# Top-k attention and Fourier mixing on one Trainium2 core: the tail tokens' product moved ahead of the seven half products, and the attention output turned by DMA and normalised on GpSimd

## The chip, the cores and the metric

The kernel runs on one core of a Trainium2 chip. The core has five engines with a queue each: TensorE (PE in the profile; its weight loads are shown as PEld), VectorE (DVE), ScalarE (ACT), GpSimd (POOL) and SyncE (SP), which in this kernel issues nearly all DMA transfers. An engine executes its own instructions in the order in which the program lists them; between engines only semaphores order the work. The metric is the device time of one execution in microseconds, and the median of several runs stands for a kernel.

## The reference

The inputs `q`, `k`, `v` have the shape (8, 8, 576, 64): batch, head, token, channel. All is float32.

```python
scores = scale * np.matmul(q, k.transpose(0, 1, 3, 2))
kth = np.partition(scores, -32, axis=-1)[..., -32:-31]
scores = np.where(scores >= kth, scores, -1e9)
attn = np.exp(scores - np.max(scores, axis=-1, keepdims=True))
attn = attn / (np.sum(attn, axis=-1, keepdims=True) + 1e-09)
x = np.matmul(attn, v)                     # then heads side by side: (8, 576, 512)
mixed = np.real(np.fft.fft(np.fft.fft(x, axis=1), axis=2))
u = x + mixed
un = (u - mean(u)) / np.sqrt(var(u) + 1e-06)
out = u + np.maximum(un @ w_ch1, 0.0) @ w_ch2        # 512 -> 2048 -> 512
```

So each batch has an attention that keeps the 32 largest scores of a row, a two-dimensional Fourier transform of which only the real part is kept, and a two-layer network.

## The kernel before, in words

**Items and steps.** Heads are handled in pairs, four pairs to a batch, 32 in all. The 576 tokens of a head are cut into tiles of 128 rows (tiles 0 and 1 of the first half, 2 and 3 of the second) and a tile 4 with the last 32 tokens of each half, 64 rows. A pair has nine items, one for each tile and head, and one for tile 4 with both heads stacked. The loop at the end of the kernel (L1492 to L1631) takes one item a step, 36 steps a batch, 288 in all. In step i the program lists: the scores of item i+3 (`scores`, L334), the finding of the 32 largest of item i on VectorE (`top_ops`, L407: four MAX8 and three MATCH_REPLACE8), the threshold on GpSimd (`bounds`, L430), the masking of item i-1 (`mask`, L445: one ScalarE pass and one GpSimd subtraction), its exponential (`expo`, L455), and the following of item i-2.

**Two ways to turn the probabilities.** The product with v needs the probabilities with keys on the partitions. For the first batch and two pairs more TensorE turns them (`transposes`, L511). For the others (`pair_by_dma`, L438: pairs 4 to 30 without 7) ScalarE writes the float32 words apart into a plane of low and a plane of high 16-bit halves (`plane`, L466), SyncE writes these to DRAM and one step later reads them back with a transposing DMA, which works on 16-bit elements (`turn`, L494). The tile `PT` that results is used one or two steps later.

**From the attention to x.** `attend` (L555) multiplies `PT` with v into one PSUM bank `o` (pool `ps_o`, a single buffer): 20 instructions for each chunk. A chunk is ch 0 (tiles 0, 1, 4; 320 columns) or ch 1 (tiles 2, 3; 256 columns), so each pair has two. The result has channels on the partitions. `attended` (L573) copies it with ScalarE to `xT` (L578) and prepares the reciprocal of the sums, `rd` (L590, L591). `to_tokens` (L594) turns `xT` with one TensorE transpose a tile (L604) into `tpx`, which takes the same bank as `o`, and multiplies by `rd` on the way into `x`: on VectorE (L608, L615), or, in batch 1 for all but its last chunk, on ScalarE in the next step (`normalise_on_act`, L627). The queue `pending` says which chunk is due; `to_tokens` may run only when the batch two before has been stored, since `x` has two buffers.

**The Fourier transform of batch b** is done among the steps of batch b+1: folds on GpSimd (`fold_ops`, `fold_tails`), products with tables (`dft_tokens`, `dft_channels`), statistics, and turning the normalised u (`channels_first`). Their steps are written out by hand (L1378 to L1438) through `at(step, place, fn)`.

**The network of batch b** is a list of units (`mlp_units`, L952) that the loop deals out among the steps of batches b+1 and b+2: each step has a budget (`level`, L1465) from an estimate of the fixed work of TensorE (`fixed_cost`, L1452), and `some` (L1482) takes units while there is room. A chunk has 16 units `hidden` (L957: eight instructions each). For the second layer there are two ways. `back` (L986) multiplies a tile plainly: eight units for a tile of 128 tokens, four for tile 4 (L1032, whose two halves of the contraction go to two halves of the output rows and are added in `tails_done`, L1041). The other way, for ch 0 of batches 1 to 6 and both chunks of batch 7, is `fast` (L1068): tiles 0 and 1 against the four quarters of `w2` in seven half-size products instead of eight, `p2, p1, p5, p4, p6, p3, p7`, two units each (L1163, 16 instructions a product). It needs sums of the hidden activations on GpSimd (`mix`, L1108) and differences of the quarters of `w2`, which lie in DRAM (`w_parts`, shown as T1 to T4) and are brought over two quarters of `w2` itself in SBUF (`bring`, L909, 512 KB for each half): `begin` brings T1 over the quarter `w2_12`, then p2 brings T4 over `w2_21`, p5 brings T2, p4 brings T3, and at last p6 and p7 bring back the quarters themselves, B12 and B21. Whatever reads `w2` plainly must come before T1 or after B12 and B21. The order of the units for such a chunk is:

```python
begin, products = fast(ch)                # products[0] is a mix, no TensorE work
units.insert(1 - NIT, begin)              # after the first hidden unit
units += products
for t in [t for t in CHUNKS[ch] if t == 4 or not seven]:      # tile 4 comes here
    units += [ ... back(ch, t, p) for p in range(4 if t == 4 else 8) ]
```

Then follow the 16 hidden units of ch 1 and the plain products of tiles 2 and 3. Results are added to `x` by GpSimd (L1135, queued in `sums` and emitted by `some_sums` as room allows) or VectorE (L1121), and stored from there. `tails_done` calls `need((b, 0, "x", 4))`, which emits the queued sums up to that one, because it reuses the space of their operand.

**Banks.** Products of the network and of the Fourier transform share three PSUM banks in a rotating list (`bank`, L130). A product of the second layer holds its bank until the VectorE operation that ends it has been listed, at the end of the next step (`late_next`).

**SyncE's queue** takes in a step: the transposing read of item i-3, the planes of item i-2, what the units bring, loads of q, k and v, stores.

Of the kernel before, what the change touches and what calls it, by code (L numbers as in the profile page):

```python
# [9 lines left out]
F32 = mybir.dt.float32  # L10
# [63 lines left out]
def kernel(  # L74
# [363 lines left out]
    def pair_by_dma(pair):  # L438

        return NPB <= pair < NPAIR - 1 and pair != 2 * NPB - 1  # L440

    def by_dma(i):
        return pair_by_dma(i // PER_PAIR)

# [128 lines left out]
    def attended(pair, ch, late):  # L573

        o, w = o_of.pop((pair, ch)), CW[ch]
        PT.pop((pair, ch))
        xT = attp.tile([P, CW[0]], F32, name=f"xT_{pair}_{ch}", tag="xT", bufs=4)
        nc.scalar.copy(out=xT[:, 0:w], in_=o[:, 0:w])  # L578
        xT_of[pair, ch] = xT
        den = den_t[pair % 3]  # L580
        if ch == 0:
            for h in range(2):
                nc.scalar.copy(
                    out=den[TH * h:TH * (h + 1), 5:6],
                    in_=den[TAIL + TH * h:TAIL + TH * (h + 1), 4:5],
                )
        c0, n = (0, 6) if ch == 0 else (6, 4)
        rd = small.tile([P, 6], F32, name=f"rd_{pair}_{ch}", tag="rd", bufs=6)

        nc.scalar.activation(out=rd[:, 0:n], in_=den[:, c0:c0 + n], func=AF.Copy, bias=1e-9)  # L590
        late.append(lambda: nc.vector.reciprocal(out=rd[:, 0:n], in_=rd[:, 0:n]))  # L591
        rd_of[pair, ch] = rd

    def to_tokens(pair, ch, at_once=True):  # L594

        b, hp = divmod(pair, NPB)
        if b not in x_of:
            x_of[b] = batp.tile([P, 5, DM], F32, name=f"x_{b}", tag="x", bufs=2)
        x = x_of[b]
        xT, rd = xT_of.pop((pair, ch)), rd_of.pop((pair, ch))  # L600
        shape, name = [P, 4, P], f"tpx_{pair}_{ch}"
        tp = ps_o.tile(shape, F32, name=name, tag="o") if at_once else bank(shape, name)
        for n, t in enumerate(CHUNKS[ch]):
            nc.tensor.transpose(tp[0:ROWS[t], n, :], xT[:, P * n:P * n + ROWS[t]], ident)  # L604
        cols = slice(P * hp, P * (hp + 1))

        def normalise():
            nc.vector.tensor_tensor(  # L608
                out=x[:, 2 * ch:2 * ch + 2, cols].rearrange("p t (e d) -> p t e d", e=2),
                in0=tp[:, 0:2, :].rearrange("p t (e d) -> p t e d", e=2),  # L610
                in1=rd[:, 0:4].rearrange("p (t e) -> p t e", e=2).to_broadcast([P, 2, 2, D]),
                op=ALU.mult,
            )
            if ch == 0:
                nc.vector.tensor_tensor(  # L615
                    out=x[0:TAIL, 4, cols].rearrange("p (e d) -> p e d", e=2),
                    in0=tp[0:TAIL, 2, :].rearrange("p (e d) -> p e d", e=2),
                    in1=rd[0:TAIL, 4:6].to_broadcast([TAIL, 2, D]),
                    op=ALU.mult,
                )  # L620

        def normalise_on_act():
            for n, t in enumerate(CHUNKS[ch]):
                r = slice(0, ROWS[t])
                for e in range(2):
                    hd = slice(D * e, D * (e + 1))
                    nc.scalar.mul(  # L627
                        out=x[r, t, cols][:, hd], in_=tp[r, n, hd],
                        mul=rd[r, 2 * n + e:2 * n + e + 1],
                    )  # L630


        if b == 1 and (hp, ch) != (NPB - 1, 1):
            at(now[0] + 1, "act", normalise_on_act)
        else:
            (late_now if at_once else late_next).append(normalise)
        return 0.14 * len(CHUNKS[ch])
# [314 lines left out]
    def mlp_units(b):  # L952
# [16 lines left out]
                )  # L969
            nc.scalar.activation(out=hT_of[ch][:, it, :], in_=hp[:, 0:w], func=AF.Relu)  # L970

        cps, cts, stored = {}, [], []

        def ct_of(t):

# [10 lines left out]
        def back(ch, t, part):  # L986
            n, hT, rs = CHUNKS[ch].index(t), hT_of[ch], rs_of[b]
            if part == 0:
                cps[t] = bank([P, DM], f"cp_{b}_{t}", True)
            cp, free = cps[t]  # L990
            if t != 4:
                for it in range(2 * part, 2 * part + 2):
                    nc.tensor.matmul(  # L993
                        cp, lhsT=hT[:, it, P * n:P * (n + 1)], rhs=w2[:, it, :],
                        start=(it == 0), stop=(it == NIT - 1),
                    )
                if part == 7:
                    xt = x[:, t, :]

                    def store():  # L1000
                        tok = HS * (t // 2) + P * (t % 2)
                        nc.sync.dma_start(out=out[b, tok:tok + P, :], in_=xt)
                        stored.append(t)
                        if len(stored) == 4:
                            written.add(b)

                    def finish():
                        nc.vector.scalar_tensor_tensor(
                            out=xt, in0=cp, scalar=rs[:, t:t + 1], in1=xt, op0=ALU.mult, op1=ALU.add
                        )  # L1010
# [12 lines left out]

                    if last:
                        store()
                    else:
                        at(now[0] + 2, "load2", store)
                return

            for it in range(2 * part, 2 * part + 2):  # L1030
                for g in range(2):
                    nc.tensor.matmul(  # L1032
                        cp[TAIL * g:TAIL * (g + 1), :],
                        lhsT=hT[:, NIT // 2 * g + it, P * n:P * n + TAIL],
                        rhs=w2[:, NIT // 2 * g + it, :],
                        start=(it == 0), stop=(it == NIT // 2 - 1),
                    )
            if part == 3:
                tails_done(cp, free)

        def tails_done(cp, free):  # L1041

            if b and not last:
                need((b, 0, "x", 4))
            ct, rs = ct_of(4), rs_of[b]
            for h in range(2):
                r0 = TAIL + TH * h
# [20 lines left out]
        def fast(ch):  # L1068
# [160 lines left out]
            def begin():  # L1229
# [2 lines left out]
                    if last:  # L1232
                        bring(T4, second, part)

            return (0.0, begin, "hidden"), [
                (0.0, lambda: mix("21", "21", "22", ALU.add), "back")
            ] + [
                (1.75, lambda f=f, part=part: f(part), "back")
# [4 lines left out]
        for ch in range(2):  # L1243
            units += [
                (8 * CW[ch] / 1200.0, lambda ch=ch, it=it: hidden(ch, it), "hidden")
                for it in range(NIT)
            ]
            seven = b and ch == 0 or last
            if seven:
                begin, products = fast(ch)  # L1250
                units.insert(1 - NIT, begin)
                units += products
            for t in [t for t in CHUNKS[ch] if t == 4 or not seven]:
                units += [
                    (1.75, lambda ch=ch, t=t, p=p: back(ch, t, p), "back")
                    for p in range(4 if t == 4 else 8)
                ]
        return units


# [191 lines left out]
    def fixed_cost(i):  # L1452

        t = 0.55 if 0 <= i - 2 < N and not by_dma(i - 2) else 0.0
        if i + 3 < N:
            t += {0: 1.04, 1: 0.3, None: 0.9}[items[i + 3][2]]
            if by_dma(i + 3) and items[i + 3][2] is not None:
                t += -0.3 if items[i + 3][2] else 0.3
        ch = chunk_at(i)[1] if i > PER_BATCH + 3 else {4: 0, 8: 1}.get((i - 3) % PER_PAIR)
        t += 0.0 if ch is None else (CW[ch] / 115.0 + 0.14 * len(CHUNKS[ch]))  # L1460
        if i < N and i % PER_PAIR in (0, 5):
            t += 0.7
        return t + costs.get(i, 0.0)
# [28 lines left out]
    while i < N + 5 or plan or queue or sums:  # L1492
# [33 lines left out]
        fixed += preps  # L1526

        tok = []

        if pending and pending[0][0] <= i and (  # L1530
            i < 2 * PER_BATCH + 4 or chunk_at(i)[0] is None
        ):
            _, pp, pc = pending[0]
            if pp // NPB < 2 or pp // NPB - 2 in written:
                pending.pop(0)
                tok.append(lambda: to_tokens(pp, pc, not short))
        if not short:
            fixed += tok
        for where in ("pe1", "pe2", "pe"):
# [83 lines left out]
        for fn in late_now:  # L1623
            fn()
        run(i, "dve")
        for where in ("pool", "pool2", "load", "load2"):
            run(i, where)
        late_now[:] = late_next
        late_next.clear()
# [38 lines left out]
```

## Time and profile before

| | us |
|---|---|
| median of three runs | 1872.15 (1869.95 to 1873.57) |
| profiled execution | 1871.9 |
| its span, first to last instruction | 1870.1 |
| TensorE matmul busy | 1702.5 (91%) |
| VectorE busy | 1580.6 (85%) |
| ScalarE busy | 1292.9 (69%) |
| GpSimd busy | 913.2 (49%) |
| DMA queue of SyncE, share of 16 engines | 50.9% |

The page of a profile gives the busy time of each engine, the span in 40 slices, the chain of work that ended last, and groups of instructions: line, engine, operation, output<-input, shapes, count, then busy time, mean duration, and the idle time of the engine just before them with what ended it. Other views of the same trace are windows (busy time of each engine, granted TensorE clock and DMA share for chosen stretches), waits (who waited for whom), and a timeline (the instructions of one engine in order; a figure in square brackets is the idle time before an instruction). A float32 product appears as two matmul instructions. Ends of matmuls are modelled, so the spacing of their starts is the better measure of what one costs.

### The profile page before, as it was taken

To read this page: it belongs to the slowest core of one execution; us is meant where nothing else is said; L and a number is where in the kernel's file an instruction comes from. 1 tells how busy PE (TensorE), PEld (TensorE's weight loads), DVE (VectorE), ACT (ScalarE), POOL (GpSimd) and SP (SyncE) were. 2 spreads that over 40 slices of the span, in tenths; PEclk is the share of its full clock that TensorE was granted. 3 is DMA by queue.
4 is the path that set the end of the run, shared out by engine and by line. 5 is a ranking of instruction groups with operands and counts; after the bars stand their busy time and mean duration, and the time that the engine had idled before them with its cause. 6 is when DMAs were issued, how large, how long until landed. Compare 5 with 4: busy or idle time off the path is not lost.

```text
span 1870.1 us, 26944 instructions
## 1 busy us (share of the span) xinstructions
PE 1702.5 (91%) x8134; PEld 1086.0 (58%) x8134; DVE 1580.6 (85%) x3301; ACT 1292.9 (69%) x3104; POOL 913.2 (49%) x1278
## 2 busy tenths in 40 slices
PE   5667699789899998999999999999999899999999
PEld 3344364355456654565566565666567555677677
DVE  7999989789899999998999899998999899863110
ACT  6878658568687778776788678867788678652100
POOL 4768643444745366354654466355545365250012
PEclk8878899899899999999999999999999999999999
DMA  5333025661467755686476755684476655530132
GB/s 168 104 98 109 20 59 157 165 168 32 121 157 191 193 134 135 154 203 152 106 176 151 211 127 133 165 223 123 120 174 173 178 126 146 133 105 1 56 104 79
DMA packets 516576, 249.16 MB, mean 133 GB/s; under 512 B 398288, under 2 KB 506448, under 8 KB 516432
## 3 DMA queue, kind: packets, MB, share of 16 engines
q1 hardware_dynamic: 515664, 247.23, 50.9%
q8 instruction: 65, 1.06, 0.2%
q14 instruction: 79, 0.65, 0.1%
q10 hardware_dynamic: 768, 0.21, 0.0%
HBM read 93.63 MB, written 84.74 MB: 95 GB/s over the span
## 4 chain that ended last, share of the span: by engine, by line
PE 50%; DVE 22%; POOL 9%; ACT 7%; issue 7%; DMA 3%; SPq 2%; POOLq 0%; DVEq 0%; ACTq 0%
PE hp L966 19%; DVE m L425 10%; DVE wk L427 10%; PE o L564 5%; PE cp L993 4%; POOL wk L451 4%; PE sp L401 4%; PE cp L1032 3%; PE cv L1163 3%; PE cw L1163 3%; ACT wk L448 2%; POOL fg L651 2%; PE yp L755 2%; DMA w<-w_parts 1%; PE sp_t L371 1%
## 5 line engine op out<-in xcount | busy, mean ns | idle before, releaser
L451 POOL TENSOR_TENSOR wk<-S,wk 128x576 f32<-128x576 f32 x288 | 409.6, 1422 | 505.8 <-ACT wk L448 504.6
L425 DVE MAX8 m<-wk 128x8 f32<-128x576 f32 x864 | 626.5, 749 | 6.0
L966 PE MATMUL hp<-unT,w 128*128 128x256 f32 (+1 forms) x2048 | 526.0, 409 | 4.7 <-ACT hT L970 4.0
L966 PEld LDWEIGHTS hp<-unT,w 128*128 128x128 f32 x2048 | 380.3, 191 | 111.1 <-issue 12.0
L427 DVE MATCH_REPLACE8 wk<-m,wk 128x576 f32<-128x576 f32 x576 | 427.6, 742 | 0.0
L472 ACT COPY wk<-S 128x576 uint16<-128x576 uint16 x468 | 289.8, 671 | 0.0
L448 ACT ACTIVATE wk<-S,nt 128x576 f32<-128x576 f32 x288 | 223.7, 777 | 87.0 <-POOL nt L434 85.7
L993 PE MATMUL cp<-w,hT 128*128 128x512 f32 x512 | 234.0, 598 | 0.0
L425 DVE MAX8 m<-S 128x8 f32<-128x576 f32 x288 | 213.8, 742 | 18.7 <-ACT S L375 18.7
L459 ACT ACTIVATE S<-wk,nt 128x576 f32<-128x576 f32 x234 | 184.2, 787 | 51.7 <-POOL wk L451 49.9
L427 DVE MATCH_REPLACE8 wk<-m,S 128x576 f32<-128x576 f32 x288 | 213.7, 742 | 0.0
L564 PE MATMUL o<-PT,v 128*64 128x256 f32 (+3 forms) x1440 | 198.4, 421 | 11.5 <-ACT x L627 6.9
L970 ACT ACTIVATE hT<-hp 128x320 f32<-128x320 f32 (+1 forms) x256 | 103.5, 413 | 141.7 <-PE hp L966 139.9
L401 PE MATMUL sp<-kT,qT 64*128 64x512 f32 (+1 forms) x528 | 172.5, 675 | 12.9 <-ACT means L1351 5.7
L564 PEld LDWEIGHTS o<-PT,v 128*64 128x64 f32 x1440 | 114.4, 155 | 87.6 <-issue 18.8
L404 ACT COPY S<-sp 128x512 f32<-128x512 f32 (+1 forms) x264 | 141.9, 587 | 31.0 <-PE sp L401 30.1
L993 PEld LDWEIGHTS cp<-w,hT 128*128 128x128 f32 x512 | 94.0, 193 | 90.3 <-issue 89.5
L1108 POOL TENSOR_TENSOR hT<-hT 128x512 f32<-128x512 f32 x64 | 81.3, 1273 | 115.6 <-ACT hT L970 97.1
L434 POOL TENSOR_TENSOR nt<-m,cc 128x2 f32<-128x2 f32 x288 | 58.1, 202 | 158.3 <-DVE m L425 157.4
L371 PEld LDWEIGHTS sp_t<-kt,qT 128*128 128x128 f32 x320 | 51.1, 195 | 112.1 <-issue 63.3
L1163 PE MATMUL cw<-w,hT 128*128 128x256 f32 x448 | 102.8, 380 | 1.7 <-POOL hT L1108 1.4
L1032 PE MATMUL cp<-w,hT 128*64 128x512 f32 x256 | 75.0, 659 | 22.6 <-DMA w<-w_parts 22.6
(160 smaller groups left out, 2156.6 us busy)
## 6 DMA issues: line engine op xcount, KB each, us to landing
planes<-wk SPq DMA_DIRECT2D x208, 288.0 KB, 2.7
w<-w_parts SPq DMA_DIRECT2D x82, 512.0 KB, 4.7
space<-in_moe_w_ch_dram SPq DMA_DIRECT2D x32, 512.0 KB, 3.7
nat<-in_q_dram SPq DMA_DIRECT2D x128, 64.0 KB, 2.4
v<-in_v_dram SPq DMA_DIRECT2D x64, 128.0 KB, 3.0
out_dram<-x SPq DMA_DIRECT2D x32, 256.0 KB, 2.6
nat<-in_k_dram SPq DMA_DIRECT2D x62, 128.0 KB, 3.0
planes<-wk SPq DMA_DIRECT2D x52, 144.0 KB, 2.7
```

What stands on the lines that cost most here:

```text
L401: nc.tensor.matmul(sp[r], lhsT=qT[hd, q_cols], rhs=kT[hd, :], start=True, stop=True)
L404: nc.scalar.copy(out=s_t[r, keys], in_=sp[r])
L425: ops.append(lambda src=src, m8=m8: nc.vector.max(out=m8, in_=src))
L427: ops.append(lambda src=src, m8=m8: nc.vector.match_replace(w, m8, src, NEG))
L448: nc.scalar.activation(out=w, in_=Ssb[i], func=AF.Relu, scale=-FAR, bias=Nt[i][:, 1:2])
L451: nc.gpsimd.tensor_tensor(out=w, in0=Ssb[i], in1=w, op=ALU.subtract)
L459: nc.scalar.activation(out=Ssb[i] if by_dma(i) else w, in_=w, func=AF.Exp, bias=Nt.pop(i)[:, 0:1], accum_out=den_t[pair % 3][:, c:c + 1],)
L472: nc.scalar.copy(out=words[:, half, :], in_=src[:, half, :])
L564: nc.tensor.matmul(o[D * e:D * (e + 1), c0:c1], lhsT=vv[:, c, e, :], rhs=pt[:, NF if c == NF else (NF + 1) * e + c, c0:c1], start=(c == 0) ...
L966: nc.tensor.matmul(hp[:, 0:w], lhsT=w1[:, dt, P * it:P * (it + 1)], rhs=unT[:, dt, 0:w], start=(dt == 0), stop=(dt == NDT - 1),)
L993: nc.tensor.matmul(cp, lhsT=hT[:, it, P * n:P * (n + 1)], rhs=w2[:, it, :], start=(it == 0), stop=(it == NIT - 1),)
L1163: nc.tensor.matmul(dst, lhsT=h()[a][:, kc, :], rhs=rhs_of(kc), start=start and kc == 0, stop=kc == NK - 1, skip_group_check=True,)
```

## The change

Part one moves tile 4's four `back` units, for the chunks that take the seven products, from behind these to in front of them. For ch 0 `begin`, the bringing of T1 (in batch 7 of T1 and T4), is no longer a unit among the hidden ones; it is called when the last of the four units of tile 4 has been listed. The call of `need` in `tails_done` goes. For ch 1 of batch 7, which has no tile 4, `begin` stays where it was. The `mix` that p5 needs is listed ahead of tile 4.

Part two concerns `attended` and `to_tokens` of the pairs that `out_by_dma` names: all that are turned by DMA, save the last pair of a batch. These are 21 pairs, three in each of the batches 1 to 7, so 42 chunks. ScalarE copies `o` in two passes, low and high halves of the words; SyncE writes the planes to DRAM (a second write for tile 4) and in `to_tokens`, at the end of the step in the new place "turn", issues a transposing read straight into `x` (a second one for tile 4). Two steps later GpSimd multiplies `x` by `rd` in place (one instruction for the two full tiles, one for tile 4). The TensorE transposes, the bank for them, and the multiplications on VectorE or ScalarE go for these chunks. Such a chunk may now be taken in a step that also has an `attend`.

Part three takes the transposes' 0.14 us a tile out of `fixed_cost` where the pair is turned by DMA, which leaves more of a step's budget for units.

```diff
+    def out_by_dma(pair, ch):
+        return pair_by_dma(pair) and pair % NPB < NPB - 1
...
         o, w = o_of.pop((pair, ch)), CW[ch]
-        xT = attp.tile([P, CW[0]], F32, name=f"xT_{pair}_{ch}", tag="xT", bufs=4)
-        nc.scalar.copy(out=xT[:, 0:w], in_=o[:, 0:w])
-        xT_of[pair, ch] = xT
+        if out_by_dma(pair, ch):
+            words = attp.tile([P, 2, CW[0]], U16, name=f"ow_{pair}_{ch}", tag="xT", bufs=4)
+            src = o[:, 0:w].bitcast(U16).rearrange("p (s h) -> p h s", h=2)
+            for half in range(2):
+                nc.scalar.copy(out=words[:, half, 0:w], in_=src[:, half, :])
+            to = xT_of[pair, ch] = dramp.tile(
+                [P, 2, CW[0]], U16, name=f"oplanes_{pair}_{ch}", tag="oplanes", bufs=6
+            )
+            nc.sync.dma_start(out=to[:, :, TAIL:], in_=words[:, :, 0:2 * P])
+            if ch == 0:
+                nc.sync.dma_start(out=to[:, :, 0:TAIL], in_=words[:, :, 2 * P:])
+        else:
...
+        if out_by_dma(pair, ch):
+            rows = xT.rearrange("p h s -> (p h) s")
+            nc.sync.dma_start_transpose(
+                out=x[:, 2 * ch:2 * ch + 2, cols].bitcast(U16), in_=rows[:, TAIL:]
+            )
+            if ch == 0:
+                nc.sync.dma_start_transpose(out=x[:, 4:5, cols].bitcast(U16), in_=rows[:, 0:P])
+            def normalise_in_place():
+                for t0, nt, n, r in ((2 * ch, 2, 0, P), (4, 1, 4, TAIL))[:2 - ch]:
+                    xs = x[0:r, t0:t0 + nt, cols].rearrange("p t (e d) -> p t e d", e=2)
+                    by = rd[0:r, n:n + 2 * nt].rearrange("p (t e) -> p t e", e=2)
+                    nc.gpsimd.tensor_tensor(
+                        out=xs, in0=xs, in1=by.to_broadcast([r, nt, 2, D]), op=ALU.mult
+                    )
+            at(now[0] + 2, "pool0", normalise_in_place)
+            return 0.0
...
             if part == 3:
                 tails_done(cp, free)
+                if begins:
+                    begins.pop()()
...
-            if b and not last:
-                need((b, 0, "x", 4))
...
                 begin, products = fast(ch)
-                units.insert(1 - NIT, begin)
-                units += products
+                if ch == 0:
+                    begins.append(begin)
+                else:
+                    units.insert(1 - NIT, (0.0, begin, "hidden"))
+                mix_first = products.pop(0)
+                units.append(mix_first)
             for t in [t for t in CHUNKS[ch] if t == 4 or not seven]:
...
+            if seven:
+                units += products
...
-        t += 0.0 if ch is None else (CW[ch] / 115.0 + 0.14 * len(CHUNKS[ch]))
+        t += 0.0 if ch is None else (
+            CW[ch] / 115.0 + (0.0 if by_dma(i - 4) else 0.14 * len(CHUNKS[ch]))
+        )
...
-            i < 2 * PER_BATCH + 4 or chunk_at(i)[0] is None
+            i < 2 * PER_BATCH + 4 or chunk_at(i)[0] is None or out_by_dma(*pending[0][1:])
...
-                tok.append(lambda: to_tokens(pp, pc, not short))
+                if not out_by_dma(pp, pc):
+                    tok.append(lambda: to_tokens(pp, pc, not short))
+                else:
+                    at(i, "turn", lambda: to_tokens(pp, pc))
...
-        for where in ("pool", "pool2", "load", "load2"):
+        for where in ("pool", "pool2", "load", "load2", "turn"):
             run(i, where)
```

More of the change, by code (lines that the diff above doesn't have):

```diff
@@ L576, in attended @@
         PT.pop((pair, ch))
-        xT = attp.tile([P, CW[0]], F32, name=f"xT_{pair}_{ch}", tag="xT", bufs=4)
-        nc.scalar.copy(out=xT[:, 0:w], in_=o[:, 0:w])
-        xT_of[pair, ch] = xT
+        if out_by_dma(pair, ch):
[10 more added lines that the diff above has]
+        else:
+            xT = attp.tile([P, CW[0]], F32, name=f"xT_{pair}_{ch}", tag="xT", bufs=4)
+            nc.scalar.copy(out=xT[:, 0:w], in_=o[:, 0:w])
+            xT_of[pair, ch] = xT
         den = den_t[pair % 3]
@@ L600, in to_tokens @@
         xT, rd = xT_of.pop((pair, ch)), rd_of.pop((pair, ch))
+        cols = slice(P * hp, P * (hp + 1))
+        if out_by_dma(pair, ch):
[14 more added lines that the diff above has]
+            return 0.0
         shape, name = [P, 4, P], f"tpx_{pair}_{ch}"
@@ L604, in to_tokens @@
             nc.tensor.transpose(tp[0:ROWS[t], n, :], xT[:, P * n:P * n + ROWS[t]], ident)
-        cols = slice(P * hp, P * (hp + 1))
         def normalise():
@@ L970, in hidden @@
             nc.scalar.activation(out=hT_of[ch][:, it, :], in_=hp[:, 0:w], func=AF.Relu)
-        cps, cts, stored = {}, [], []
+        cps, cts, stored, begins = {}, [], [], []
         def ct_of(t):
@@ L1233, in begin @@
                         bring(T4, second, part)
-            return (0.0, begin, "hidden"), [
+            return begin, [
                 (0.0, lambda: mix("21", "21", "22", ALU.add), "back")
```

## The prediction

> **What bounds the kernel now.** I first read the windows by batch. Columns: stretch, length, busy time (instructions) of PE, PEld, DVE, ACT and POOL, granted clock, DMA share, GB/s.
>
> ```profile
> 628.00:812.00 184.00, 172.96 (x845) 105.59 (x843) 181.60 (x380) 146.76 (x351) 91.77 (x141) 0.99 0.57 143
> 1017.00:1222.00 205.00, 199.29 (x970) 126.16 (x968) 191.73 (x401) 157.78 (x378) 105.21 (x155) 0.98 0.62 159
> ```
>
> There are two regimes. From 628 on VectorE never waits: 34 first MAX8 (one a step) in 650 to 830 make 5.29 us a step, 190.6 us for 36 steps. From 830 to 1660 a batch takes 204.8 us (the same stall recurs at 1050.23, 1255.05 and 1460.61); TensorE is busy nearly all of it, VectorE is idle for 13.3 us a batch. So there TensorE sets the pace, and I read its timeline: start, length, operation, instructions, and in brackets the idle time before.
>
> ```profile
> 1245.84 3.62 PE L1163 MATMUL cw<-w,hT 128*128 128x256 f32 x16
> 1249.38 1.07 PE L1032 MATMUL cp<-w,hT 128*64 128x512 f32 x2
> 1255.05 3.67 PE L1032 MATMUL cp<-w,hT 128*64 128x512 f32 x6 [4.59 <-DMA w<-w_parts]
> 1258.65 1.33 PE L308 MATMUL tpq<-ident,nat 128*128 128x128 f32 x5
> 1259.91 2.41 PE L1032 MATMUL cp<-w,hT 128*64 128x512 f32 x8
> 1262.15 2.86 PE L564 MATMUL o<-PT,v 128*64 128x320 f32 x20
> ```
>
> After p7 the tail's product waits for B21. Then six of its instructions take 3.67 us, where later eight take 1.87 (0.234 each): that is the clock. The fine windows show it in the third column from the end:
>
> ```profile
> 1252.00:1256.00 4.00, 0.95 (x4) 0.34 (x5) 3.97 (x9) 0.00 (x0) 0.19 (x1) 0.76 1.09 344
> 1256.00:1260.00 4.00, 4.00 (x13) 1.44 (x11) 3.93 (x8) 0.20 (x1) 0.00 (x0) 0.50 0.84 209
> 1264.00:1270.00 6.00, 6.00 (x36) 2.06 (x34) 0.76 (x2) 3.96 (x13) 0.00 (x0) 1.00 0.70 191
> ```
>
> VectorE stays full during the stall and starves just after it (0.76 of 6 us). SyncE's timeline says why the data are late:
>
> ```profile
> 1246.96 0.56 SPq L909 DMA_DIRECT2D w<-w_parts  x1
> 1247.57 1.26 SPq L288 DMA_DIRECT2D v<-in_v_dram  x2
> 1248.87 1.17 SPq L255 DMA_DIRECT2D v<-in_v_dram  x2
> 1250.15 0.59 SPq L485 DMA_DIRECT2D planes<-wk  x1
> 1250.84 1.16 SPq L909 DMA_DIRECT2D w<-w_parts  x2
> ```
>
> B21 stands behind the loads of v, is issued some 3 us after p7's first half was read, and lands 4.2 us later. DMA share is above 1.0.
>
> **The tail's product first.** At full clock its first eight instructions and the tpq group cost 8 x 0.234 + 0.55 = 2.42 us, the next eight 1.87: 4.29. From 1249.38 to 1262.32 they took 12.94, so the stall costs 8.6 us. The same sum at the other places gives 10.0 (838.35 to 852.65), 8.4 (1044.66 to 1057.34) and 8.9 (1454.17 to 1467.33); batch 1 lost 2.7, batch 6 0.3. All: **38.9 us**. All of it goes, since the tails then read `w2` before T1. What is late next: (a) p5 needs T1, now begun only after the tail. p2 starts at 1217.60 and p5 at 1228.30, 10.7 us later; SyncE's lag of 0 to 3 us and a landing of 4.7 (3.7 to 8.1 for L909) make 5 to 11. Mostly hidden; I take 1 us in all, bounds 0 and 6 x 3 = 18. (b) Plain products after the seven now have 16 hidden units (28 us) before them: B12 and B21 are hidden. (c) Hidden units now follow p7 directly, while p3 and p7 still hold two of the three banks to the end of the next step; one unit or so has a single bank and waits for the ScalarE copy. Nearest row: matmuls L966 waiting for ACT hT, 4.0 us in 3 waits, 1.3 each. 6 batches x 1 unit x 1.3 = 8 us; bounds 0 and three units, 23. In batch 7 `begin` for ch 0 was early and is now late; four halves of 512 KB have the 6.9 us of p2 and p1 to land. Taken as 0, bounds 0 and 5.
>
> **The output by DMA.** The rows for what goes, and for the nearest to what comes:
>
> ```profile
> L604 PE MATMUL tpx<-ident,xT 128*128 128x128 f32 x128 | 25.2, 279 | 5.7 <-ACT xT L578 4.0 <-DVE x L615 1.6
> L608 DVE TENSOR_TENSOR x<-tpx,rd 128x256 f32<-128x256 f32 x57 | 23.9, 420 | 27.2 <-PE tpx L604 24.5 <-DVE rd L591 0.5
> L578 ACT COPY xT<-o 128x320 f32<-128x320 f32 x32 | 13.7, 428 | 2.9 <-PE o L564 2.3
> L1135 POOL TENSOR_TENSOR x<-x,ct 128x256 f32<-128x256 f32 x30 | 21.7, 732 | 6.8 <-ACT ct L1133 6.7
> ```
>
> TensorE: 21 pairs x 5 transposes = 105, spaced 0.11 us (three in 0.33 in the chain), **11.5 us**, 1.65 a batch. VectorE: 18 pairs x (2 x 0.42 + 0.27) = 20.0 us, 3.3 a batch, and its waits for tpx (9.7 us in 628 to 1631). Batch 1: 30 ScalarE multiplications of 0.33 us go, and with them a hold on the `o` bank:
>
> ```profile
> 305.97 4.54 PE L564 MATMUL o<-PT,v 128*64 128x256 f32 x20 [2.91 <-ACT x L627]
> ```
>
> Two such waits make 6.9 us, and here the clock was 0.50 in 306 to 312: 4.54 instead of 2.31 and 1.88 instead of 1.13 for the scores, 3.0 more. Of these 9.9 us I count 3, since TensorE is busy for only 176.5 of 203 us of 220 to 423.
>
> What comes. ScalarE: a second copy for 42 chunks at 0.43 or 0.39, 17 us; the 16-bit copy L472 (576 elements, 0.671) suggests the same price an element. Bounds 17 and, if strided reading of PSUM doubles both, 52. It is busy for 77% of a batch, so I count 1 us, bounds 0 and 10. GpSimd: 42 x 0.73 (L1135) + 21 x 0.45 (64x127 fold) = 40 us, 5.8 a batch, beside 100 us idle: 0 in itself; its waits are the rival below. SyncE: 63 writes x 0.57, and 63 transposing reads between 0.37 (shortest plain issue) and 2.5 (L506, nine blocks where these have two or one), 0.8 taken: 86 us, 12 a batch. The writes follow ScalarE copies of the first part of their step, and the reads stand at a step's end, behind a write of the step before (2.7 us to landing): I count 1 us, bounds 0 and 10. DMA: 12 MB more on 249.
>
> Two pages speak against this. The Trainium skill, "DMA: Bandwidth & Descriptors", Specifications, wants at least 512 B a piece, or the write becomes read-modify-write; the tail's write has pieces of 128 B. In the trace the 16 KB loads of v in pieces of 256 B land in 2.5 us and the 128 KB ones in 3.0; were the new tail write to need double, 5 us, it would still land before its read. The skill's "TensorE: Matmul & The Clock Gate", What's actually happening, halves the clock after an idle window of about 3.4 us; the 2.91 us wait above was already followed by 0.50, so the row decides: by the rule a new 3 us wait costs 3, by the row about 6.
>
> **The sum.** A TensorE-bound batch goes from 204.8 to 204.8 - 8.5 - 1.65 = 194.6. VectorE's floor falls to 190.6 - 3.3 = 187.3, so TensorE stays the bound and VectorE is no limit. Where the two alternate some of it will be lost; VectorE idles 6.1 us a batch beyond the stall's 7.2, and I let 2 us a batch go. Batches 2 to 5: 4 x (10.2 - 2) = 33. Batch 1's stall and the VectorE-bound stretch: 4 (3.3 and a little of 2.7). Batch 6: 2. The bank of batch 1: 3. Together 42; costs 1 + 8 + 1 + 1 = 11. The planner's smaller `fixed_cost` shifts units by 0.4 us a step: 0. So -31 us on the profiled 1871.9: **1841**. That run is within 0.3 us of the median, so I forecast 1841 us.
>
> **Rivals.**
> - *Floors hold, nothing lost:* 38.9 + 11.5 + 9.9 = 60 us is the whole of it, 1812; likelier with half of my losses, 1820. For: TensorE idles almost only in this stall. Against: VectorE full in 1382 to 1426 (43.5 of 44).
> - *The wait moves to p5:* T1 crowds a window with a DMA share of 1.1, 3 us late in six batches, twice with the slow clock: 18 + 5, 1864. Against: the 10.7 us.
> - *Banks and ScalarE:* three hidden units a batch on one bank, 23 instead of 8: 1856.
> - *Slower:* GpSimd, whose queue is in order, stands at the new multiplication waiting for the transposing read; behind it are `bounds` and the next mask, thus ScalarE and the scores. Time allowed: one to two steps, 5.3 to 10.6 us. Needed in the crowded window: lag 3 + landing 4.6 (3.3 to 9.6) = 7.6. It decides from 31 / 42 = 0.74 us exposed a chunk; at 1.5 us it costs 63: 1904. Against: GpSimd waits for ScalarE anyway (73 us in 1222 to 1426).
>
> **Numbers.** Forecast 1827 to 1852: 0.38. Floors 0.17, p5 0.13, banks 0.14, slower 0.14, near nothing 0.04. Differences under 0.2% (3.7 us) can't be told from none. Faster 0.82, same 0.04, slower 0.14. The range 1812 to 1868 holds all but the last two.
>
> **What will show it.** Right: L1032 without a DMA wait, no 0.50 windows past 630, batches of 194 to 198 us, tpx with 55 transposes. Wrong: L1163 waiting for w_parts, L966 waiting for ACT hT by over 10 us, or the new GpSimd line waiting for a DMA ahead of `bounds`.

## The result, and the profile after

| us | before | after |
|---|---|---|
| median of 5 runs | 1872.85 (1869.95 to 1877.33) | 1864.42 (1860.76 to 1868.64) |
| ratio | 1 | 0.9956 (95%: 0.9941 to 0.9971) |
| profiled execution / its span | 1871.9 / 1870.1 | 1864.42 / 1862.6 |
| TensorE, VectorE busy | 1702.5, 1580.6 | 1687.7, 1568.4 |
| ScalarE, GpSimd busy | 1292.9, 913.2 | 1299.0, 943.8 |
| share of SyncE's DMA queue | 50.9% | 54.9% |

The change makes the kernel 8 us faster, not the 31 forecast. The instructions went as it says: TensorE executes 8029 matmuls instead of 8134, 105 fewer. The groups of the changed kernel (its numbers of lines are 4 to 35 higher: the product L1163 is now L1197, `tpx` L604 is L639, `bring` L909 is L943, the read of planes L506 is L510, the tail's product L1032 is L1066):

```profile
L639 PE MATMUL tpx<-ident,xT 128*128 128x128 f32 x44 | 8.8, 281 | 4.0 <-ACT xT L594 3.9
L585 ACT COPY ow<-o 128x320 uint16<-128x320 uint16 x42 | 15.8, 429 | 0.5
L630 POOL TENSOR_TENSOR x<-x,rd 128x256 f32<-128x256 f32 x42 | 25.7, 613 | 3.3 <-DMA x<-oplanes 3.2
L1197 PE MATMUL cw<-w,hT 128*128 128x256 f32 x448 | 111.5, 400 | 22.5 <-DMA w<-w_parts 21.1
```

The first three rows are part two: fewer transposes, two 16-bit copies a chunk at the price of the old one, and GpSimd's multiplication, which waited only 3.2 us for its data. The fourth is where the gain went: products of the seven wait 21.1 us in all for blocks of `w2` (20.4 of it is p6 in batches 2 to 5); before they waited 0.2. The tail's product L1066 has no wait for a DMA any more. In the windows (columns as in the prediction) the stretch of batch 4 is as full as before, and the half clock is still there, at 1245 to 1250 instead of 1256 to 1260:

```profile
1017.00:1222.00 205.00, 198.74 (x971) 125.98 (x968) 193.20 (x398) 162.13 (x391) 111.99 (x168) 0.99 0.66 169
1245.00:1250.00 5.00, 3.81 (x10) 2.66 (x10) 4.93 (x11) 0.00 (x0) 0.07 (x1) 0.50 1.17 307
```

TensorE's timeline of the changed kernel at this place:

```profile
1232.75 3.62 PE L1197 MATMUL cv<-w,hT 128*128 128x256 f32 x16
1236.20 3.62 PE L1197 MATMUL cw<-w,hT 128*128 128x256 f32 x16
1246.18 3.75 PE L1197 MATMUL cw<-w,hT 128*128 128x256 f32 x8 [6.37 <-DMA w<-w_parts]
```

These are p5, p4 and p6. p6 needs T2, which may be brought only when p5 has read the space. So T2 has the rest of p5 and all of p4 as cover: the second half of p5, 1.7 us, and 3.45 for p4, together 5.2. Before, the scores, the transposes of k and another `tpx` group stood in between, and the cover was 7.4. SyncE's timeline shows when T2 is issued:

```profile
1228.32 3.57 SPq L240 DMA_DIRECT2D nat<-in_q_dram  x4
1232.00 1.25 SPq L279 DMA_DIRECT2D nat<-in_q_dram  x2
1233.84 1.71 SPq L1093 DMA_DIRECT2D out_dram<-x  x2
1235.60 1.21 SPq L620 DMA_TRANSPOSE x<-oplanes  x1
1236.85 2.81 SPq L510 DMA_TRANSPOSE PT<-planes  x1
1239.78 1.23 SPq L492 DMA_DIRECT2D planes<-wk  x2
1241.10 1.14 SPq L943 DMA_DIRECT2D w<-w_parts  x2
```

T2 stands last in a row of loads of q, the tails' stores (moved here by part one), a read of x (part two), a read of planes and two writes. SyncE issues them almost without a pause, so T2 is issued 6.6 us after p5's first half was read at 1234.5; before, 1.8 us after (at 1231.84). Call this the lag, the time from issue to arrival the landing (4.9 us for this block), and the time that TensorE has other work the cover. Lag 6.6 plus landing 4.9 less cover 5.2 makes 6.3, and the wait is 6.37. The same sum as in the prediction's first step (starts less their spacing at full clock) gives for p6 7.7, 6.2, 8.9 and 6.4 us in batches 2 to 5: **29.2 us of the 38.9 came back**, as a wait of the same kind for another block. How much is the queue's and how much the load on the DMA engines' cannot be read from this alone: the median block took 5.0 us from issue to landing after and 4.7 before.

The last batch lost 3 us. From the end of the hidden units of ch 0 to the end of the span it takes 90.8 us, 87.7 before: T1 is now issued when the tail's product has been listed, behind the stores, at 1782.62, and p5 waits for it twice.

```profile
1786.83 1.97 PE L1197 MATMUL cv<-w,hT 128*128 128x256 f32 x8 [0.84 <-DMA w<-w_parts]
1790.29 1.97 PE L1197 MATMUL cv<-w,hT 128*128 128x256 f32 x8 [1.49 <-DMA w<-w_parts]
```

### The profile page after: what moved, and what is told of

Its sections match the earlier page's. It is cut to its first block, busy times and chain, and to the rows that moved or that the text cites. A ratio compares the mean times of both kernels' runs of the same rounds, so it can differ in the third digit from the quotient of the medians.

```text
span 1862.6 us, 26953 instructions
## 1 busy us (share of the span) xinstructions
PE 1687.7 (91%) x8029; PEld 1081.1 (58%) x8029; DVE 1568.4 (84%) x3247; ACT 1299.0 (70%) x3116; POOL 943.8 (51%) x1341
## 3 DMA queue, kind: packets, MB, share of 16 engines
q1 hardware_dynamic: 561696, 260.32, 54.9%
## 4 chain that ended last, share of the span: by engine, by line
PE 57%; DVE 16%; ACT 9%; POOL 7%; issue 5%; DMA 5%; SPq 1%; POOLq 0%; DVEq 0%
PE hp L1000 20%; DVE wk L427 7%; DVE m L425 7%; PE cp L1027 6%; PE o L568 6%; PE sp L401 4%; PE cw L1197 4%; PE cv L1197 4%; PE yp L789 3%; POOL wk L455 3%; DMA w<-w_parts 2%; PE cp L1066 2%; ACT wk L452 2%; PE sp_t L371 2%; ACT wk L476 1%
## 5 line engine op out<-in xcount | busy, mean ns | idle before, releaser
L401 PE MATMUL sp<-kT,qT 64*128 64x512 f32 (+1 forms) x528 | 172.1, 678 | 13.2 <-ACT means L1391 5.7
L404 ACT COPY S<-sp 128x512 f32<-128x512 f32 (+1 forms) x264 | 141.8, 587 | 47.6 <-PE sp L401 46.9
L1197 PE MATMUL cw<-w,hT 128*128 128x256 f32 x448 | 111.5, 400 | 22.5 <-DMA w<-w_parts 21.1
L1197 PEld LDWEIGHTS cw<-w,hT 128*128 128x128 f32 x448 | 86.9, 199 | 38.8 <-POOL nt L434 15.9
```

The costliest lines, as they stand in the source:

```text
L401: nc.tensor.matmul(sp[r], lhsT=qT[hd, q_cols], rhs=kT[hd, :], start=True, stop=True)
L404: nc.scalar.copy(out=s_t[r, keys], in_=sp[r])
L1197: nc.tensor.matmul(dst, lhsT=h()[a][:, kc, :], rhs=rhs_of(kc), start=start and kc == 0, stop=kc == NK - 1, skip_group_check=True,)
```

## The experiments

Theory Q: SyncE's queue, in order, is late for T2, and every microsecond it has to issue ahead of T2 comes back in the wait. Rival D: the DMA engines are full, and landings got later with the bytes. Part S asks what the second part of the change is worth. A ratio below is against the kernel before, run beside it (medians 1872.4 to 1873.93).

**Each part alone.** First `out_by_dma` returning `False`, with the old `fixed_cost`; then the old order of the units, with the output by DMA.

> Only the tail's product is moved ahead of the seven; the output stays as before (TensorE transposes, no new DMA, fixed_cost as before). Cover theory: the wait only changes its place. p6 needs T2, which may be brought only once p5 has read T1, and between p5 and p6 stands only p4 with 3.45 us, where a landing takes 5 us and SyncE's lag comes on top; so L1163-like waits of p6 for w_parts of 4 to 6 us stay in batches 2 to 5 without any of the new DMA work, 25 to 35 us with the slow clock, and the time is 1862 to 1870 us. Queue theory: T2 is late because the new writes and transposing reads of the output stand ahead of it on SyncE; without them p6 waits under 1 us and the time is 1838 to 1848 us.

> Only the output goes by DMA (with the smaller fixed_cost); the tail's product stays behind the seven and T1 early. If the two parts are independent: the stall of the tail for B21 stays at 36 us, the transposes give 11.5 us and the bank of batch 1 about 3, so 1856 to 1862 us. If the new DMA work delays B21 or T2 further: over 1866 us, with longer waits of the tail or of p6 for w_parts.

Part one alone: 1861.07 us, ratio 0.9931 (0.9908 to 0.9954). Parts two and three alone: 1865.66, 0.9961 (0.9948 to 0.9973). They gain 12.7 and 8.1 us, and together only 8.4 (against the 1872.85): the parts harm each other. The views put 8.6 us of waits down to `w_parts` in the first, 21.1 with part two beside it, but these names mislead. In batch 4 of part one alone p6 starts so:

```profile
1246.09 3.54 PE L1197 MATMUL cw<-w,hT 128*128 128x256 f32 x8 [1.90 <-ACT S L404]
```

p6 reads nothing that L404 writes; T2 was issued at 1241.04 and landed 4.9 us later, at 1245.9. So this too is a wait for T2: lag 3.7 plus landing 4.9 less cover 6.7 (here scores and a transposed score product stand between p4 and p6) makes 1.9. Whatever name they carry, the waits in front of p6's two halves in batches 2 to 5 add up to 15.1 us in part one alone and 20.4 in the changed kernel. (One of them, 2.5 us in batch 2 of part one alone, ended as both GpSimd's sum and T2 arrived.) By the sum of starts p6 loses 24.3 us against 29.2. So most of the stall moved to p6 by the new order alone, as the cover theory had it (25 to 35 us, and a time of 1862 to 1870, both missed by about 1 us); the queue theory's "under 1 us" without the new DMA work is refuted. Part two's DMA work adds some 5 us. In the second kernel the tail's product waits 22.1 us (22.6 before), so the gain there is not the stall's; its time lies between the two ranges.

**Other work ahead of p6.** p3, which needs nothing of T2, goes ahead of p6:

```diff
-                for f in (p2, p1, p5, p4, p6, p3, p7) for part in range(2)
+                for f in (p2, p1, p5, p4, p3, p6, p7) for part in range(2)
```

> The changed kernel with p3 listed ahead of p6 (and the store of the first tile behind p6), so T2 has p4 and p3, 6.9 us, to land, and T3 has p3 and p6 as before. Cover theory: p6's wait falls from 4.5 to 6.4 us to under 2 in batches 2 to 5, the clock stays up, and some 25 of 29 us come back: 1836 to 1846 us. Queue theory: the lag of 4.7 plus a landing of 5 is 9.7 us, so 2 to 3 us of wait a batch stay: 1848 to 1856 us. If VectorE or something else takes over as the bound: p6 does not wait, but the time stays above 1856 us.

1860.33 us, 0.9923 (0.9906 to 0.9941). The wait of `cw` for `w_parts` is all but gone (1.7 us), and its gain was mostly spent again; the time is above 1856, the third case of the expectation. This is from the waits of this kernel (line waited for, total, times, longest):

```profile
PE o L568 <- DMA PT<-planes: 21.5, 8, 4.8
```

It was 9.0 us in 3 waits in the changed kernel. Hiding one late transfer uncovered the next that SyncE issues in this stretch.

**A space of its own for T2.** Its first half goes into a buffer of the Fourier folds that is free then, issued right behind T1; the second half follows the first half of p5, and B12 goes behind p6. The same was done on part one alone.

```diff
+                own.append(batp.tile([P, NK // 2, DH], F32, name=f"own_{b}_{ch}", tag="fold_d"))
+                nc.sync.dma_start(out=own[0], in_=scr[:, T2, 0:NK // 2, :])
...
-                bring(T2, w2_12, part)
+                if part == 0:
+                    nc.sync.dma_start(out=w2_12[:, 0:NK // 2], in_=scr[:, T2, NK // 2:NK, :])
```

> The changed kernel with the first half of T2 brought at once behind T1 into space of its own (the folds' scratch, free at that time), and the second half over the first half of T1 as soon as p5's first part has read it; B12 comes back behind p6. The order of the products is as in the change. Cover theory: p6's first part never waits and the second has 6.9 us of cover, so the wait vanishes as with p3 ahead: 1836 to 1846 us. If the transfers themselves are the bound (DMA share over 1.1 in this stretch), the wait moves once more, to p5 for T1 or p4 for T4: over 1852 us.

> The tail's product ahead of the seven and T2's first half in space of its own, but the output as before (TensorE transposes, VectorE). If the output by DMA is worth its transposes once T2 is not late: this is slower than e4_t2_own_space by about 10 us, 1857 to 1865 us. If the output by DMA costs more SyncE time than it saves: this is equal or faster, 1840 to 1851 us.

1851.28 us (1844.81 to 1858.02), 0.9877 (0.9854 to 0.9899), with 8.1 us of waits for `w_parts` left, now in front of p6's second half; and on part one alone 1852.86, 0.99 (0.9878 to 0.9922). Both times fall between the ranges of their expectations. With T2 out of the way part two is worth 1.6 us, less than the runs can tell.

**More ahead of T2.** Four loads of 1.5 KB that nothing uses, all to one small tile, then a single one of 512 KB, in batches 1 to 6:

```diff
+                if part == 0 and not last:
+                    for _ in range(4):
+                        nc.sync.dma_start(out=idle_t, in_=sg_d.ap())
```

```diff
+                if part == 0 and not last:
+                    spare = batp.tile([P, NK // 2, DH], F32, name=f"spare_{b}", tag="fold_d")
+                    nc.sync.dma_start(out=spare, in_=scr[:, T2, 0:NK // 2, :])
```

> The changed kernel with four loads of 1.5 KB into unused space on SyncE directly ahead of T2's first half, in batches 1 to 6: some 0.5 us of SyncE each, no bytes to speak of. Queue theory (T2 is late because SyncE's in-order issue is behind): p6's waits for w_parts grow from 4.5 to 6.4 by about 2 us each, and the time by 8 to 14 us. Engine theory (T2 is late because the 16 DMA engines are full): waits and time as in the change, 1860 to 1868 us.

> The changed kernel with one load of 512 KB into unused space on SyncE directly ahead of T2's first half, in batches 1 to 6: 0.55 us of SyncE, and some 2 us of all 16 DMA engines at the 250 GB/s of this stretch. Queue theory: p6's waits grow by 0.5 us each, the time by 2 to 5 us. Engine theory: they grow by 2 us or more each, the time by 8 to 14 us.

With four small loads 1886.42 us, 1.0075 (1.0057 to 1.0094), 22 more than the changed kernel. They took more of SyncE than I had meant. Each takes 0.33 us to issue and lands 1.7 us later, and all write one tile, so each waited for the one before. SyncE's and TensorE's timelines of this kernel in batch 4:

```profile
1254.35 6.11 SPq L1232 DMA_DIRECT2D idle<-c_sg  x4
1260.55 0.94 SPq L944 DMA_DIRECT2D w<-w_parts  x2
```

```profile
1264.71 3.75 PE L1198 MATMUL cw<-w,hT 128*128 128x256 f32 x8 [9.89 <-DMA w<-w_parts]
```

Some 6 KB of data, but 6.1 us of the queue: p6 waits 9.89 us instead of 6.37, and the waits add up to 39.1. That speaks for Q. One load of 512 KB costs SyncE 0.60 us and gives 1871.78 us, 0.9999 (0.9989 to 1.0008), 7.4 more, between the ranges of the two theories; the waits are 23.6, which is 0.7 us more for each p6 of batches 2 to 5, nearer to Q's 0.5 than to D's 2. So bytes may count too, but 512 KB cost a third of what 6.1 us of the queue cost. The sum holds for the small loads too: lag 11.1, landing 4.0, cover 5.2 make 9.9.

**Less ahead of T2.** The tails' stores of batches 1 to 6 are issued six steps later:

```diff
-                for h in range(2):
-                    tok = HS * h + 2 * P
...
+                if seven_first:
+                    at(now[0] + 6, "load2", store_tails)
+                else:
+                    store_tails()
```

> The changed kernel with one edit: the tails' stores of batches 1 to 6 are issued 6 steps later. They took some 1.7 us of SyncE just ahead of the issue of T2 in batch 4. Queue theory: the wait of p6 for w_parts falls by 1.5 to 2.3 us in each of batches 2 to 5, and the time by 6 to 10 us, to 1854 to 1858 us. DMA-load theory: the same bytes in the same stretch, so within 2 us of 1864.42.

1851.2 us, 0.9885 (0.9871 to 0.99): 13.2 us less from twelve short instructions, with the same bytes moved, and more than Q had expected. In batch 4 T2 is issued 1.2 us after p4's start, 4.9 before the edit. It is more than the stores' own 1.7 us a batch, since the queue also stood 0.6 us in front of them, and the loads of q ahead took 2.1 instead of 3.6. Waits of this kernel, then p6 in batch 4:

```profile
PE cw L1205 <- DMA w<-w_parts: 8.6, 3, 4.0
```

```profile
1239.93 1.97 PE L1205 MATMUL cw<-w,hT 128*128 128x256 f32 x8 [2.36 <-ACT wk L476]
```

Here too a wait for T2 carries another name: lag 2.9 plus landing 4.7 less cover 5.2 makes 2.4. Counted so, the waits in front of p6 in batches 2 to 5 are 13.4 us instead of 20.4, and three of the four batches lose no time to the slow clock any more. By the sum of starts p6 loses 16.4 us instead of 29.2, that is 12.8 less, and the time is 13.2 less. Batch 2 gained nothing. D alone allowed 2 us; and at the price of the 512 KB load the 128 KB of a batch's two stores would be worth 1.9 us in all.

**Writes on ScalarE's queue.** On the kernel with T2 in its own space: the 63 writes of the output's planes issued by ScalarE, the later stores, and batch 7 in the old order.

```diff
-            nc.sync.dma_start(out=to[:, :, TAIL:], in_=words[:, :, 0:2 * P])
+            nc.scalar.dma_start(out=to[:, :, TAIL:], in_=words[:, :, 0:2 * P])
```

> e4_t2_own_space with less on SyncE in the crowded stretch: the planes of the output are written from ScalarE's queue, the stores of the tail come six steps later, and batch 7 keeps the old order with T1 and T4 early. Queue theory: the waits left in e4 (8.1 us for w_parts, 9.0 for PT) shrink to under 8 together and batch 7 gets back 3 us: 1834 to 1844 us. If ScalarE is now too full to issue: 1848 us or more, with longer waits on ScalarE's copies.

1870.17 us, 0.9985 (0.9973 to 0.9996): 19 slower than without these edits. An issue costs ScalarE 0.56 to 0.63 us, 63 of them 35 to 40, and the product `mp` now waits 9.9 us for ScalarE. Here the writes are dearer on ScalarE than on SyncE.

**The two cures together,** with and without part two: T2 in its own space, later stores, batch 7 in the old order.

> The kernel with T2 in a space of its own, and in it the tails' stores of batches 1 to 6 put 6 steps later in SyncE's queue, and batch 7 in the order of the kernel before. Queue theory (what is lost is what SyncE has to issue ahead of the tail's blocks): the 8.1 us that the first product with T2 still waited for w_parts fall below 3, the last batch gives back 3, so 1840 to 1850 us against 1851.28 without the two edits. Theory that the DMA engines' load sets it: the same bytes are moved, so 1849 to 1854 us, with the waits on w_parts and planes where they were.

> The same two edits on the kernel with the attention's output as before (part one of the change alone, T2 in a space of its own; 1852.86 us without them). Beside the run above it, this gives the price of the attention's output by DMA where no product waits for the tail's blocks. If TensorE sets the stretch, the transposes' 11.5 us come back here and this kernel is 5 to 12 us slower than the one above (1850 to 1858 us); if ScalarE's 55 second copies or SyncE's 25 reads cost as much as the transposes give, the two are within 3 us of each other.

With part two **1838.64 us**, 0.9815 (0.9798 to 0.9832): the best kernel here, and 1 us under Q's range. Without it 1839.67, 0.9825 (0.9812 to 0.9838). The intervals overlap: part two is worth nothing that can be told, even with hardly a product waiting for `w2`. (It has 42 second copies and 63 transposing reads of `x`, not the 55 and 25 of the expectation.) The window of the first, for the stretch shown above:

```profile
1017.00:1222.00 205.00, 202.56 (x995) 129.89 (x992) 198.28 (x407) 166.18 (x400) 112.65 (x168) 1.00 0.70 179
```

TensorE is busy for 202.56 of 205 at full clock: no long stall is left. From the first MAX8 of one item to that of the item a batch later (items 150, 186, 222 and 258) it takes 197.7, 197.5 and 196.2 us (204.7, 204.8, 205.2 before; 203.0, 203.9, 201.5 in the changed kernel), and without part two 197.8, 197.7 and 196.2.

**What part two gives and takes.** In the stretch of batches 3 to 5 the 45 transposes cost TensorE 4.9 us by the spacing of their starts, 0.11 each as forecast. With part two TensorE's waits from 1017 to 1629 add up to 9.1 us, without it to 5.8: 2.2 us more stand in front of the seven products and 1.8 more in front of `mp`, which waits for `y` from ScalarE. The difference, 3.3 us, takes back two thirds of the 4.9. Theories: the transposes are worth nothing there; or ScalarE's second copies take back what they give. Three edits: the transposes made twice (without part two), the first copy made once more (on the best kernel), the two copies joined.

```diff
-            nc.tensor.transpose(tp[0:ROWS[t], n, :], xT[:, P * n:P * n + ROWS[t]], ident)
+            for _ in range(2 if b and hp < 3 else 1):
+                nc.tensor.transpose(tp[0:ROWS[t], n, :], xT[:, P * n:P * n + ROWS[t]], ident)
```

```diff
-            for half in range(2):
+            for half in (0, 0, 1):
                 nc.scalar.copy(out=words[:, half, 0:w], in_=src[:, half, :])
```

> The kernel that has the attention's output as before (TensorE turns it), T2 in its own space and the later stores (1839.67 us), with the 105 transposes of the pairs in question made twice. Theory one (TensorE sets the stretch, and taking the transposes out was worth their 0.11 us each; ScalarE's second copies took it back): 8 to 12 us slower, 1848 to 1852 us. Theory two (TensorE's time there is absorbed by the waits for ScalarE that follow, so the transposes were worth nothing): within 3 us of 1839.67.

> The same kernel (1838.64 us) with the first of the two copies made once more, 42 instructions, some 17 us of ScalarE; the result stays the same. Theory one (ScalarE's second copy costs what the transposes gave): 6 to 17 us slower, 1845 to 1856 us. Theory two (ScalarE has room): within 3 us of 1838.64.

> The kernel with the output by DMA, T2 in its own space and the later stores (1838.64 us), with ScalarE's two copies of each chunk joined into one instruction over both halves (42 instructions fewer). The two took 0.80 us together for ch 0 and fewer for ch 1; if what an instruction costs to start is some 0.1 to 0.2 us, 4 to 8 us of ScalarE go. Theory one (ScalarE's copies are on the path): 2 to 5 us faster, 1834 to 1837 us. Theory two (ScalarE has room): within 2 us of 1838.64.

> The changed kernel with the first of ScalarE's two copies of each transposed chunk made once more (55 instructions of about 0.37 us, some 17 to 20 us of ScalarE in all; the result stays the same). If the second copy lies on the path that sets the end, this is 8 to 20 us slower than the changed kernel (1872 to 1884 us); if ScalarE has room there, it is within 3 us of 1864.42.

The last of the four is the third copy on the changed kernel (42 instructions, not the 55 that its expectation says). Results: transposes twice 1846.57, 0.9853 (0.984 to 0.9867), 6.9 us slower for 11.5 us of TensorE; third copy 1857.94, 0.9912 (0.9899 to 0.9926), **19.3 us slower** for 16.0 of ScalarE; third copy on the changed kernel 1871.43, 0.999 (0.9976 to 1.0003), 7.0 slower for 17.8, where the p6 wait shrank to 14.4 at the same time. The first and the last fall between the ranges, the second above its own. So neither is worth nothing, and a copy's time is the dearer one here, though the third copy also holds back the write of the planes behind it. With it TensorE's waits in the stretch grow from 9.1 to 17.0 us, 3.8 of it in front of the seven products and 2.5 in front of `mp`. One place in batch 4 shows how a copy can cost more than it lasts. TensorE's timeline of the kernel with three copies:

```profile
1136.96 0.71 PE L846 MATMUL mp<-fd,y 128*128 128x128 f32 x4 [1.87 <-ACT y L825]
1137.51 1.87 PE L850 MATMUL mp<-fd,y 128*128 128x256 f32 x4
1139.17 2.77 PE L1028 MATMUL cp<-w,hT 128*128 128x512 f32 x4
```

and in the best kernel:

```profile
1131.08 0.71 PE L846 MATMUL mp<-fd,y 128*128 128x128 f32 x4 [1.04 <-ACT y L825]
1131.63 1.03 PE L850 MATMUL mp<-fd,y 128*128 128x256 f32 x4
1132.50 1.88 PE L1028 MATMUL cp<-w,hT 128*128 128x512 f32 x4
```

ScalarE comes 0.83 us later with `y`; then eight instructions take 4.64 us instead of 2.91. So 0.83 us of delay cost 2.6; the granted clock in the window of the kernel with three copies is 0.63:

```profile
1138.00:1142.00 4.00, 4.00 (x10) 2.20 (x9) 2.71 (x6) 4.00 (x11) 1.19 (x1) 0.63 1.07 259
```

The joined copies gave 1842.39, 0.9831 (0.9817 to 0.9844), 3.8 us slower with overlapping intervals, and tell nothing: a joined copy lasts 0.69 or 0.62 us, and two single ones 0.75 or 0.68 from the first's start to the second's end, so only some 2.5 us of ScalarE were saved in all.

## Why the prediction was wrong, point by point

The range held the time; the forecast of 1841 us did not.

- **The tail's stall, 38.9 us, "All of it goes": the step that failed.** The stall left the tail's product as forecast, and 29.2 us of it stood in front of p6, 24.3 with part one alone. "What is late next" was asked for T1 and p5, for B12 and B21, not for T2 and p6, though with the seven products back to back only p4 lies between the space coming free and p6, and the prediction itself put the queue's lag at up to 3 us. With the prediction's own numbers, lag 3 plus landing 4.7 less cover 5.2 would have been 2.5 us in each of four batches; in batch 4 the lag was 6.6. Of the forecast 31 us, 29.2 went to p6 and 3 to the last batch, and the 8 counted for single banks did not come: if the other terms held, that leaves 7, and 8 were measured.
- **SyncE, counted 1 of 0 to 10:** mis-sized, though within its bounds. Its price is paid at p6, which with part two loses 29.2 us instead of 24.3 (first experiment). What else stands in the queue counts as well: two stores a batch moved aside give 13.2 us back. A transposing read of x took 1.21 us of the queue where 0.8 was taken.
- **T1 for p5, 1 us:** right in batches 1 to 6, where p5 hardly waited. **Batch 7, taken as 0 of 0 to 5:** 3 us.
- **Hidden units on one bank, 8 us:** not there; these units waited 1.7 us for ScalarE in the whole run, 4.0 before.
- **TensorE's transposes:** 0.11 us each was right; doubling them costs 6.9 for 11.5 us, so 60% of it counts. **ScalarE's second copies, counted 1 of 0 to 10:** the same number of copies more costs 19.3 us where no stall hides them, so 1 was probably too little; what the second copies themselves cost was not measured. Part two's other gains (VectorE's 20 us, and the bank of batch 1: item 60 comes 3.5 us earlier than before in the best kernel and 0.6 later in the same without part two) stand against it; how they share was not measured and stays open.
- **GpSimd as the slower rival:** refuted, 3.2 us in two waits. It multiplies in 0.61 and 0.39 us, not 0.73 and 0.45.
- **The p5 rival at 1864:** the right time by the wrong block. Its mechanism, a transfer of the seven that crowds the same window, was the right kind, and the sign named for it (L1163 waiting for `w_parts`) is what appeared.
- **Losses of 2 us a batch and VectorE's floor:** consistent with the best kernel: its batches of 196 to 198 us are the forecast 194 to 198. The forecast's sum is reached once T2, the stores and batch 7 are mended, at 1838.64 us, though not by its terms alone.

The skill's rule on the clock was weighed against a row of 2.91 us. The third copy's row goes further: 1.87 us of waiting were followed by a window at 0.63, and a wait of 1.04 us by one at 1.00. But in the kernel with the later stores waits of 2.36, 2.42 and 2.96 us in front of p6 were followed by windows at 1.00, so the length of one wait does not decide alone. The Trainium skill, "TensorE: Matmul & The Clock Gate", What's actually happening, puts the idle window at some 3.4 us; these rows show a lower clock after less.

## What to carry to other kernels

When a stall on a transfer is removed by changing the order, ask of every later transfer in the chain what it now has for cover, and subtract the in-order queue's lag at that very place, not on average. Moving instructions out of the queue ahead of the one transfer that is due was worth more here than the whole change (13.2 us for twelve stores, against 8.4). When a view names what ended a wait, check that the instruction reads it; here waits for T2 stood under ScalarE's name. Time freed on the busiest engine counted in part (6.9 us for 11.5), and time put on an engine with 30% idle counted in full or more (19.3 for 16.0), where it delayed that engine's answer to the busiest one.

## What the runs showed of the hardware

- In the rows shown, a transposing DMA keeps SyncE's queue for 1.2 us (reads of x, one or two blocks) to 2.8 us (PT, nine blocks); plain ones for 0.6 to 0.9 each.
- Issued by ScalarE, a write costs that engine 0.56 to 0.63 us.
- A ScalarE copy of 16-bit halves out of PSUM with a stride of two words' halves lasts as long as the float32 copy of as many elements: 0.429 and 0.428 us for 128x320.
- TensorE ran at 0.63 in a window after 1.87 us of waiting, and at 1.00 after 2.96 us in another kernel.
